# A leftover expert pair at the end of a fused attention and MoE kernel: its steps between the last units, its last rows added on chip

## The chip, the cores and the metric

One core of a Trainium2 chip. The core has TensorE (PE, with its weight loads PEld), VectorE (DVE), ScalarE (ACT), GpSimd (POOL) and SyncE (SP); DMAs are issued from queues of SP, POOL and ACT. The metric is the device time of one execution in microseconds (us).

## The reference

```python
# attention with one key/value head: q (8, 16, 384, 64), k and v (8, 1, 384, 64)
scores = (q @ k.T) / sqrt(64)
attn   = softmax(scores)                 # over the keys
x      = (attn @ v) -> (3072, 1024)      # 8 batches x 384 tokens, 16 heads x 64
# gated experts: 4 groups x 4 experts, w1 and w2 are 1024 x 1024 each
g = argmax(x @ w_group);     g_w = softmax(x @ w_group)[g]
e = argmax(x @ w_expert[g]); e_w = softmax(x @ w_expert[g])[e]
out[token] = g_w * e_w * (relu(x[token] @ w1[g, e]) @ w2[g, e])
```

Each token goes to one of 16 experts.

## The kernel before

The attention runs in 24 rounds, one for each 128 query tokens (8 batches of 384 tokens, so three rounds to a batch); the kernel's order is written out by hand and is the order of the instructions on each engine.

For every batch the kernel picks the expert that most of its first 128 tokens chose, loads that expert's w1 and w2 (POOL queue), and runs **all** 384 tokens of the batch through it, with a gate of zero for tokens that chose another. This work is cut into **units** (`moe_units`): 8 h units (w1, 8 matmuls of 384 columns, then Relu on ACT, lines L407 and L408), and 6 y units (w2, 8 matmuls of 512 columns at L415, then on ACT the eviction with the gate as scale at L416). A y unit makes 128 tokens by half of the 1024 output columns; after the second half the 128 rows are stored by SP (L436, 512 KB). `fill(n)` puts the next n units into the order; they fill PE between the attention's steps. The last batch's units come after the attention.

A pair (batch, expert) that some tokens chose, but that was not the batch's pick, is a **leftover**. `early_pair` (L508 on) finds the first such pair before the last batch is done, and its weights are loaded ahead (`leftover_w1`, `leftover_w2`, L544). Up to 32 of its tokens (`CAP`) are then done at the end:

- the batch's x is read back from DRAM (`xe`, L626), the tokens' ranks come from a prefix matmul (`pr`), and one-hot matrices `pick` (128 tokens by 32 ranks, repeated four times over 128 columns, fp32) are made (L653). `pg` (L659) gathers the gate and the token number of each rank; `gc` and `rows` (L661 to L664) are the gate and the row of the scatter, for four quarters of the output row on four groups of 32 partitions
- `pb` transposes (L681) and copies `xt` give x with tokens on the partitions; three of the last units stand between them
- `px` (L692) gathers the 32 tokens, `xc` is its copy on DVE; `ph` (L700) multiplies by w1, `hg` is its Relu on ACT (L702); `phT` (L705) transposes, `hc` is the copy on DVE (L707); `py` (L712) multiplies by w2, `yc` is the scaled copy on ACT (L714), 128 partitions (4 quarters by 32 tokens) by 256 columns
- POOL scatters `yc` to the rows of the output with an indirect DMA (L715). It waits until every earlier store to the output has landed, as it overwrites their zeros.

In before all remaining units are put ahead of `px`:

```python
    fill(len(units) - 1)
    rare = nc.values_load(rarei[0:1, 0:1], ...)
    fill(1)
    px = side([P, KO, CAP], FP32, "px")
```

`rare` (one load into a register on each engine) says whether more pairs are left or the softmax bound failed; it is zero in the profiled execution (none of the lines behind it ran), and a branch at L767 skips that part on each engine to the program's end (L858, where SP waits for all queues and the engines meet in barriers). SP waits at L767 until all its stores have landed, POOL until its DMAs have.

PSUM tiles of `side` come from a pool of three buffers in turn; `ps_m` has one, the attention's accumulator `o`.

Of the kernel before, what the change touches and what calls it, by code (L numbers as in the profile page):

```python
# [9 lines left out]
FP32 = mybir.dt.float32  # L10
# [3 lines left out]
P = 128  # L14
ACTF = mybir.ActivationFunctionType
OP = mybir.AluOpType
# [5 lines left out]
def kernel(  # L22
# [11 lines left out]
    nc = tc.nc  # L34
    B, H, S, D = q.shape
    N, Dm = out.shape
# [5 lines left out]
    ST = S // P  # L42
    KO = Dm // P
    FO = F // P
    GE = G * Eg
    scale = 1.0 / (D ** 0.5)
    NCH = 6
    CW = 512
    NFLAT = B * NCH
    NPAIR = B * GE  # L50
    CAP = 32
    QW = Dm // 4
# [4 lines left out]
    out4 = out.rearrange("n (q c) -> (n q) c", q=4)  # L57
# [18 lines left out]
    def side(shape, dtype, name):  # L76
        return ps_s.tile(shape, dtype, tag="s", name=name)
# [317 lines left out]
        nc.vector.reduce_sum(out=gs[:], in_=gm[:], axis=AX)  # L395
        gsel[b] = gs

    def moe_units(w1, w2, xb, gs_of, place, store):
        units = []
        state = {}  # L400

        def h_unit(fc):
            if fc == 0:
                state["h"] = pool.tile([P, FO, S], BF16, tag="hT", bufs=1, name="hT")
            ps = side([P, CW], FP32, "hps")
            for ko in range(KO):
                nc.tensor.matmul(out=ps[:, 0:S], lhsT=w1[:, ko, fc * P:(fc + 1) * P], rhs=xb[:, ko, :], start=(ko == 0), stop=(ko == KO - 1))  # L407
            nc.scalar.activation(out=state["h"][:, fc, :], in_=ps[:, 0:S], func=ACTF.Relu)  # L408

        def y_unit(st, nh):  # L410
            cs = slice(nh * CW, (nh + 1) * CW)
            y = place(st, cs)
            ps = side([P, CW], FP32, "yps")
            for fo in range(FO):
                nc.tensor.matmul(out=ps[:], lhsT=state["h"][:, fo, st * P:(st + 1) * P], rhs=w2[:, fo, nh * CW:(nh + 1) * CW], start=(fo == 0), stop=(fo == FO - 1))  # L415
            nc.scalar.activation(out=y, in_=ps[:], func=ACTF.Copy, scale=gs_of()[:, st:st + 1])  # L416
            store(st, cs, y)

        for fc in range(FO):
            units.append(lambda fc=fc: h_unit(fc))  # L420
        for st in range(ST):
            for nh in range(2):
                units.append(lambda st=st, nh=nh: y_unit(st, nh))
        return units

    def first_units(b):
        rows = {}

        def place(st, cs):
            if cs.start == 0:  # L430
                rows[st] = pool.tile([P, Dm], FP32, tag="y", bufs=4, name="y")
            return rows[st][:, cs]

        def store(st, cs, y):
            if cs.stop == Dm:
                nc.sync.dma_start(out=outv[b, :, st, :], in_=rows[st][:])  # L436
        return moe_units(wts[b][0], wts[b][1], xbf[b], lambda: gsel[b], place, store)

    NP = B * ST

# [10 lines left out]
    def fill(n):  # L451
        while n > 0:
            if not units:
                if begun[0] >= B or begun[0] not in wts:
                    return
                units.extend(first_units(begun[0]))
                begun[0] += 1
            units.pop(0)()
            n -= 1
            ran[0] += 1  # L460
            if ran[0] == (FO + 2 * ST) * (B - 2) + FO:
                leftover_w1()
            if ran[0] == (FO + 2 * ST) * (B - 1):
                leftover_w2()
# [43 lines left out]
    def early_pair():  # L508
        last = B - 1
        mask = pool.tile([P, GE], FP32, tag="mask", bufs=1, name="mask1")  # L510
        idf = pool.tile([P, 1], FP32, tag="idf", bufs=1, name="idf1")
        nc.vector.tensor_copy(out=idf[:], in_=choice[last][:, 0:1])
        nc.vector.tensor_scalar(out=mask[:], in0=iota16[:], scalar1=idf[:, 0:1], scalar2=None, op0=OP.is_equal)
        nc.vector.scalar_tensor_tensor(out=extra[:, last * GE:NPAIR], in0=seen[last], scalar=0.0, in1=mask[:], op0=OP.is_gt, op1=OP.subtract)
        known = pool.tile([P, 1], FP32, tag="known", bufs=1, name="known")
        nc.vector.reduce_sum(out=known[:], in_=extra[:], axis=AX)
        top = pool.tile([P, 8], FP32, tag="top", bufs=1, name="top2")
        idx = pool.tile([P, 8], U32, tag="idx2", bufs=1, name="idx2")
        nc.vector.max_with_indices(out_max=top[:], out_indices=idx[:], in_=extra[:])
        pf = pool.tile([P, 1], FP32, tag="pf", bufs=1, name="pf")  # L520
        nc.vector.tensor_copy(out=pf[:], in_=idx[:, 0:1])
        base = pool.tile([P, 1], U32, tag="base", bufs=1, name="base")
        nc.vector.tensor_scalar(out=base[:], in0=idx[:, 0:1], scalar1=NPAIR - GE, scalar2=None, op0=OP.bitwise_and)
        basef = pool.tile([P, 1], FP32, tag="basef", bufs=1, name="basef")
        nc.vector.tensor_scalar(out=basef[:], in0=base[:], scalar1=float(S // GE), scalar2=None, op0=OP.mult)
        gi = pool.tile([P, ST, 2], FP32, tag="gi", bufs=1, name="gi")
        nc.vector.tensor_scalar(out=gi[:, :, 1], in0=tokid[:], scalar1=basef[:, 0:1], scalar2=None, op0=OP.add)
        reg = nc.values_load(idx[0:1, 0:1], engines=(ET.Pool, ET.DVE, ET.SP), min_val=0, max_val=NPAIR - 1, skip_runtime_bounds_check_because="an index into 128 flags")
        leftover.update(known=known, pf=pf, gi=gi, reg=reg)

    def parts_of(pair):
        e_reg = nc.s_assert_within(pair & (GE - 1), 0, GE - 1, skip_runtime_bounds_check_because="the bits of an index below 128")
# [130 lines left out]
    rows = pool.tile([P, 1], U32, tag="rows", bufs=1, name="rows")  # L663
    nc.vector.tensor_copy(out=rows[:], in_=gc[:, 1:2])  # L664

    nc.vector.tensor_sub(out=small[:, 1:2], in0=nfl[:], in1=small[:, 0:1])
    nex = pool.tile([1, 1], I32, tag="nex", bufs=1, name="nex")
    nc.vector.tensor_copy(out=nex[:], in_=small[0:1, 1:2])
# [9 lines left out]
    for st in range(ST):  # L678
# [4 lines left out]
        nc.vector.tensor_copy(out=xt[:], in_=pb[:])  # L683
        xtok.append(xt)
        fill(1)
    fill(len(units) - 1)
    rare = nc.values_load(rarei[0:1, 0:1], min_val=0, max_val=2, skip_runtime_bounds_check_because="a sum of two comparisons")
    fill(1)
    px = side([P, KO, CAP], FP32, "px")
    for ko in range(KO):  # L690
        for st in range(ST):
# [1 line left out]
    xc = pool.tile([P, KO, CAP], BF16, tag="qT", bufs=2, name="xc")  # L693
    nc.vector.tensor_copy(out=xc[:], in_=px[:])

    w1c, w2c = leftover["w1"], leftover["w2"]
    ph = side([P, QW], FP32, "ph")
    for ko in range(KO):
# [1 line left out]
            nc.tensor.matmul(out=ph[CAP * g:CAP * g + CAP, :], lhsT=xc[:, ko, :], rhs=w1c[:, ko, g * QW:(g + 1) * QW], start=(ko == 0), stop=(ko == KO - 1), tile_position=(0, CAP * g))  # L700
    hg = pool.tile([P, QW], BF16, tag="pt", bufs=9, name="hg")
    nc.scalar.activation(out=hg[:], in_=ph[:], func=ACTF.Relu)  # L702
    phT = side([P, 2, P], BF16, "phT")
    for h in range(2):
        nc.tensor.transpose(out=phT[:, h, :], in_=hg[:, h * P:(h + 1) * P], identity=ident_bf[:])  # L705
    hc = pool.tile([P, 2, P], BF16, tag="qT", bufs=2, name="hc")
    nc.vector.tensor_copy(out=hc[:], in_=phT[:])  # L707
    py = side([P, QW], FP32, "py")
    for g in range(4):
        for h in range(2):  # L710
# [1 line left out]
                nc.tensor.matmul(out=py[CAP * c:CAP * c + CAP, :], lhsT=hc[:, h, CAP * g:CAP * g + CAP], rhs=w2c[:, 2 * g + h, c * QW:(c + 1) * QW], start=(g == 0 and h == 0), stop=(g == 3 and h == 1), tile_position=(0, CAP * c))  # L712
    yc = pool.tile([P, QW], FP32, tag="pt", bufs=9, name="yc")
    nc.scalar.activation(out=yc[:], in_=py[:], func=ACTF.Copy, scale=gc[:, 0:1])  # L714
    nc.gpsimd.indirect_dma_start(out=out4, out_offset=bass.IndirectOffsetOnAxis(ap=rows[:], axis=0), in_=yc[:], in_offset=None, bounds_check=4 * N - 1, oob_is_err=False)  # L715

    def load_pair(pair):
        e_reg, b_reg = parts_of(pair)
# [144 lines left out]
```

## Time and the profile before

| what | us |
|---|---|
| median of 3 runs | 462.71 (462.43 to 462.92) |
| the profiled execution | 463.58 |
| its span, first to last instruction | 462.0 |
| PE busy in the span | 450.8 |
| ScalarE, VectorE, GpSimd busy | 242.6, 305.7, 60.4 |
| first matmul of the last 6 y units | 439.85 |
| first matmul of px | 450.21 |
| start of the scatter on POOL | 455.58 |

The span is cut into 40 slices on the page; the clock granted to TensorE was 0.994 of full speed over the span. Durations of rows are one execution's. Ends of matmuls are modelled, so consecutive rows of PE overlap a little. A letter q behind an engine's name (SPq, POOLq) means its sequencer: branches, semaphore instructions, DMA issues.

### The profile page before, as it was taken

To read this page: it belongs to the slowest core of one execution; us is meant where nothing else is said; L and a number is where in the kernel's file an instruction comes from. 1 tells how busy PE (TensorE), PEld (TensorE's weight loads), DVE (VectorE), ACT (ScalarE), POOL (GpSimd) and SP (SyncE) were. 2 spreads that over 40 slices of the span, in tenths; PEclk is the share of its full clock that TensorE was granted. 3 is DMA by queue.
4 is the path that set the end of the run, shared out by engine and by line. 5 is a ranking of instruction groups with operands and counts; after the bars stand their busy time and mean duration, and the time that the engine had idled before them with its cause. 6 is when DMAs were issued, how large, how long until landed. Compare 5 with 4: busy or idle time off the path is not lost. (4 is left out here: it accounts for less than half of the span.)

```text
span 462.0 us, 10131 instructions
## 1 busy us (share of the span) xinstructions
PE 450.8 (98%) x4191; PEld 199.3 (43%) x4191; DVE 305.7 (66%) x483; ACT 242.6 (53%) x351; POOL 60.4 (13%) x83
## 2 busy tenths in 40 slices
PE   8999999999999999999999999999999999999992
PEld 6333444333533445343533435343443535344641
DVE  3999967964879286973779475992779564764400
ACT  2967645636366454745366364745457363623331
POOL 1004003000031002100030001300030000330000
PEclk9999999999999999999999999999999999999997
DMA  7697996998479691996759684996749712799981
GB/s 150 94 153 106 216 215 103 198 252 181 78 116 210 212 191 29 195 226 157 153 88 210 182 163 101 174 234 140 163 90 207 171 47 91 121 212 260 286 218 61
DMA packets 152165, 74.56 MB, mean 161 GB/s; under 512 B 120216, under 2 KB 138652, under 8 KB 152112
## 3 DMA queue, kind: packets, MB, share of 16 engines
q0 software_dynamic: 28416, 37.84, 47.2%
q1 hardware_dynamic: 122368, 35.68, 32.5%
q8 instruction: 35, 0.57, 0.5%
q10 hardware_dynamic: 1328, 0.33, 0.4%
q14 instruction: 18, 0.15, 0.1%
HBM read 92.62 MB, written 19.01 MB: 242 GB/s over the span
## 5 line engine op out<-in xcount | busy, mean ns | idle before, releaser
L253 ACT ACTIVATE pt<-s 128x1024 f32<-128x1024 f32 x144 | 142.1, 1026 | 67.2 <-PE s L251 66.4
L251 PE MATMUL s<-qT,kT 64*64 64x512 f32 x1152 | 142.8, 595 | 0.2 <-ACT qT L229 0.2
L290 PE MATMUL o<-pt,v 64*64 64x512 f32 x1152 | 141.0, 590 | 0.0
L261 DVE TENSOR_TENSOR presum<-presum,pt 128x1024 f32<-128x1024 f32 x96 | 116.6, 1215 | 16.3 <-ACT pt L253 10.9
L407 PE MATMUL hps<-xbf,w 128*128 128x384 bf16 x512 | 87.4, 326 | 0.0
L415 PE MATMUL yps<-w,hT 128*128 128x512 bf16 x384 | 85.4, 379 | 0.6 <-ACT y L416 0.6
L290 PEld LDWEIGHTS o<-pt,v 64*64 64x64 f32 x1152 | 43.5, 133 | 76.9 <-issue 73.2
L259 DVE TENSOR_TENSOR presum<-pt 128x1024 f32<-128x1024 f32 x24 | 29.4, 1224 | 69.3 <-ACT pt L253 68.5
L251 PEld LDWEIGHTS s<-qT,kT 64*64 64x64 f32 x1152 | 40.2, 133 | 64.3 <-issue 52.2
L416 ACT ACTIVATE y<-yps,gsel 128x512 f32<-128x512 f32 x48 | 32.6, 686 | 61.9 <-PE yps L415 49.9
L407 PEld LDWEIGHTS <-w 128*128 128x128 bf16 x512 | 48.6, 98 | 35.7 <-issue 4.1
L301 POOL CAST xbf<-xT 128x1024 bf16<-128x1024 f32 x24 | 25.0, 1041 | 280.8 <-DVE xT L300 280.8
L408 ACT ACTIVATE hT<-hps 128x384 bf16<-128x384 f32 x64 | 31.3, 488 | 51.0 <-PE hps L407 44.0
L415 PEld LDWEIGHTS <-hT 128*128 128x128 bf16 x384 | 36.8, 98 | 47.7 <-issue 4.9
L145 POOL DMA_DIRECT2D w<-in_moe_w_dram x36 | 24.8, 708 | 77.8 <-issue 58.7
L300 DVE TENSOR_TENSOR xT<-o,rinv 128x1024 f32<-128x1024 f32 x24 | 29.2, 1215 | 3.7 <-PE o L290 3.7
L280 DVE STREAM_TRANSPOSE rinv<-rc 128x1024 f32<-128x1024 f32 x24 | 29.9, 1245 | 0.8
L265 DVE TRANSPOSE_TENSOR_REDUCE fold<-presum 128x32 f32<-128x1024 f32 x24 | 29.6, 1232 | 0.0
L243 DVE STREAM_TRANSPOSE qT<-qraw 128x1024 f32<-128x1024 f32 x20 | 24.1, 1202 | 0.0
L209 ACT ACTIVATE qraw<-qraw 128x1024 f32<-128x1024 f32 x21 | 22.0, 1049 | 0.0
L318 DVE STREAM_TRANSPOSE L<-gps 128x32 f32<-128x32 f32 (+1 forms) x16 | 3.6, 227 | 17.4 <-PE gps L312 17.4
L273 PEld LDWEIGHTS sm<-fold,sel 64*64 64x64 f32 x192 | 7.2, 133 | 12.9 <-issue 12.9
(143 smaller groups left out, 158.2 us busy)
## 6 DMA issues: line engine op xcount, KB each, us to landing
w<-in_moe_w_dram POOLq DMA_DIRECT2D x36, 512.0 KB, 10.1
w<-in_moe_w_dram POOLq DMA_DIRECT2D x9, 2048.0 KB, 21.6
out_dram<-y SPq DMA_DIRECT2D x24, 512.0 KB, 2.8
qraw<-in_q_dram SPq DMA_DIRECT2D x56, 192.0 KB, 3.8
x_bf<-xbf SPq DMA_DIRECT2D x8, 768.0 KB, 4.6
v<-in_v_dram SPq DMA_DIRECT2D x16, 96.0 KB, 2.9
k<-in_k_dram SPq DMA_DIRECT2D x28, 48.0 KB, 2.6
qn<-in_q_dram SPq DMA_DIRECT2D x4, 256.0 KB, 5.0
```

Of the source, the lines that this page charges most:

```text
L251: nc.tensor.matmul(out=ps[64 * c:64 * c + 64, a, :], lhsT=kT[b][r, j * D:(j + 1) * D], rhs=qT[p][r, c * CW:(c + 1) * CW], start=True, stop ...
L253: nc.scalar.activation(out=t[:], in_=ps[:], func=ACTF.Exp, scale=scale)
L259: nc.vector.tensor_add(out=presum[p][:], in0=pt[p, 0][:], in1=pt[p, 1][:])
L261: nc.vector.tensor_add(out=presum[p][:], in0=presum[p][:], in1=pt[p, j][:])
L265: nc.vector.tensor_reduce(out=fold[p][:], in_=presum[p][:].rearrange("p a (n i) -> p (a n) i", i=32), axis=AX, op=OP.add, apply_transpose= ...
L280: nc.vector.transpose(out=t[:].rearrange("p (b i) -> p b i", i=32), in_=rc[:].rearrange("p c b -> p (c b)").unsqueeze(2).to_broadcast([P, ...
L290: nc.tensor.matmul(out=o_ps[p][64 * a:64 * a + 64, c, :], lhsT=v_sb[b][r, j, :], rhs=pt[p, j][r, a, :], start=(j == 0), stop=(j == KB - 1))
L300: nc.vector.tensor_mul(out=xT[b][:, :, ts], in0=o_ps[p][:].rearrange("p c (h n) -> p (c h) n", n=P), in1=rinv[p][:].rearrange("p (h n) -> ...
L407: nc.tensor.matmul(out=ps[:, 0:S], lhsT=w1[:, ko, fc * P:(fc + 1) * P], rhs=xb[:, ko, :], start=(ko == 0), stop=(ko == KO - 1))
L408: nc.scalar.activation(out=state["h"][:, fc, :], in_=ps[:, 0:S], func=ACTF.Relu)
L415: nc.tensor.matmul(out=ps[:], lhsT=state["h"][:, fo, st * P:(st + 1) * P], rhs=w2[:, fo, nh * CW:(nh + 1) * CW], start=(fo == 0), stop=(fo ...
L416: nc.scalar.activation(out=y, in_=ps[:], func=ACTF.Copy, scale=gs_of()[:, st:st + 1])
```

## The change

- `px` and what follows stand between the last six y units: `px`, unit 0, `ph`, unit 1, `phT`, units 2 and 3, `py`, unit 4, the rest, unit 5. The copies on DVE and ACT (`xc`, `hg`, `hc`, `yc`) are then beside a unit.
- The scatter is issued after `py`, and covers only the first 3072 - 128 tokens; so it waits for the stores up to units 2 and 3, not for the last one. The register load of `rare` comes after it on POOL.
- For the last 128 tokens (those of units 4 and 5) the leftover's rows are added on chip. `final` (in `early_pair`) is 1 where the leftover's batch is the last. `of_last` is `pick` of the batch's last 128 tokens times `final`, and is transposed on PE into the free part of `pg`'s tile and copied back by DVE, ahead of the rare flag's small steps. `spread()` stands between the matmuls of unit 4 and those of unit 5: four fp32 matmuls put the rows of `yc` back to their token (zero for other tokens), and ACT copies them to SBUF (`yl`). Units 4 and 5 are no longer evicted by ACT, but by one VectorE instruction each: PSUM times gate plus `yl`.
- Units 4 and 5 are stored in two halves of 256 KB (L437 of after).

```diff
--- before.py
+++ after.py
@@ -395,7 +395,7 @@
         nc.vector.reduce_sum(out=gs[:], in_=gm[:], axis=AX)
         gsel[b] = gs
 
-    def moe_units(w1, w2, xb, gs_of, place, store):
+    def moe_units(w1, w2, xb, gs_of, place, store, merge=None):
         units = []
         state = {}
 
@@ -413,7 +413,8 @@
             ps = side([P, CW], FP32, "yps")
             for fo in range(FO):
                 nc.tensor.matmul(out=ps[:], lhsT=state["h"][:, fo, st * P:(st + 1) * P], rhs=w2[:, fo, nh * CW:(nh + 1) * CW], start=(fo == 0), stop=(fo == FO - 1))
-            nc.scalar.activation(out=y, in_=ps[:], func=ACTF.Copy, scale=gs_of()[:, st:st + 1])
+            if merge is None or not merge(st, cs, ps, y):
+                nc.scalar.activation(out=y, in_=ps[:], func=ACTF.Copy, scale=gs_of()[:, st:st + 1])
             store(st, cs, y)
 
         for fc in range(FO):
@@ -432,9 +433,33 @@
             return rows[st][:, cs]
 
         def store(st, cs, y):
-            if cs.stop == Dm:
+            if closes(st):
+                nc.sync.dma_start(out=outv[b, :, st, cs], in_=y)
+            elif cs.stop == Dm:
                 nc.sync.dma_start(out=outv[b, :, st, :], in_=rows[st][:])
-        return moe_units(wts[b][0], wts[b][1], xbf[b], lambda: gsel[b], place, store)
+
+        def closes(st):
+            return b == B - 1 and st == ST - 1
+
+        def merge(st, cs, ps, y):
+            if not closes(st):
+                return False
+            if cs.start == 0:
+                spread()
+            nc.vector.scalar_tensor_tensor(out=y, in0=ps[:], scalar=gsel[b][:, st:st + 1], in1=leftover["y"][:, cs], op0=OP.mult, op1=OP.add)
+            return True
+        return moe_units(wts[b][0], wts[b][1], xbf[b], lambda: gsel[b], place, store, merge)
+
+    def spread():
+        lo = [ps_m.tile([P, 2, CW], FP32, tag="o", name="lo"), side([P, 2, CW], FP32, "lo2")]
+        for i in range(2):
+            for c in (i, 2 + i):
+                r = slice(CAP * c, CAP * c + CAP)
+                nc.tensor.matmul(out=lo[c // 2][:, c % 2, 0:QW], lhsT=leftover["spread"][r, :], rhs=leftover["yc"][r, :], start=True, stop=True, tile_position=(CAP * c, 0))
+        t = pool.tile([P, Dm], FP32, tag="pt", bufs=9, name="yl")
+        for i in range(2):
+            nc.scalar.copy(out=t[:, i * CW:(i + 1) * CW].rearrange("p (c n) -> p c n", c=2), in_=lo[i][:, :, 0:QW])
+        leftover["y"] = t
 
     NP = B * ST
 
@@ -525,8 +550,10 @@
         nc.vector.tensor_scalar(out=basef[:], in0=base[:], scalar1=float(S // GE), scalar2=None, op0=OP.mult)
         gi = pool.tile([P, ST, 2], FP32, tag="gi", bufs=1, name="gi")
         nc.vector.tensor_scalar(out=gi[:, :, 1], in0=tokid[:], scalar1=basef[:, 0:1], scalar2=None, op0=OP.add)
+        final = pool.tile([P, 1], FP32, tag="final", bufs=1, name="final")
+        nc.vector.tensor_scalar(out=final[:], in0=base[:], scalar1=float(NPAIR - GE), scalar2=None, op0=OP.is_equal)
         reg = nc.values_load(idx[0:1, 0:1], engines=(ET.Pool, ET.DVE, ET.SP), min_val=0, max_val=NPAIR - 1, skip_runtime_bounds_check_because="an index into 128 flags")
-        leftover.update(known=known, pf=pf, gi=gi, reg=reg)
+        leftover.update(final=final, known=known, pf=pf, gi=gi, reg=reg)
 
     def parts_of(pair):
         e_reg = nc.s_assert_within(pair & (GE - 1), 0, GE - 1, skip_runtime_bounds_check_because="the bits of an index below 128")
@@ -663,6 +690,12 @@
     rows = pool.tile([P, 1], U32, tag="rows", bufs=1, name="rows")
     nc.vector.tensor_copy(out=rows[:], in_=gc[:, 1:2])
 
+    of_last = pool.tile([P, 2, P], FP32, tag="presum", bufs=1, name="of_last")
+    nc.vector.tensor_scalar(out=of_last[:, 0, :], in0=pick[:, ST - 1, :], scalar1=leftover["final"][:, 0:1], scalar2=None, op0=OP.mult)
+    nc.tensor.transpose(out=pg[:, P:2 * P], in_=of_last[:, 0, :], identity=ident[:])
+    nc.vector.tensor_copy(out=of_last[:, 1, :], in_=pg[:, P:2 * P])
+    leftover["spread"] = of_last[:, 1, :]
+
     nc.vector.tensor_sub(out=small[:, 1:2], in0=nfl[:], in1=small[:, 0:1])
     nex = pool.tile([1, 1], I32, tag="nex", bufs=1, name="nex")
     nc.vector.tensor_copy(out=nex[:], in_=small[0:1, 1:2])
@@ -683,9 +716,7 @@
         nc.vector.tensor_copy(out=xt[:], in_=pb[:])
         xtok.append(xt)
         fill(1)
-    fill(len(units) - 1)
-    rare = nc.values_load(rarei[0:1, 0:1], min_val=0, max_val=2, skip_runtime_bounds_check_because="a sum of two comparisons")
-    fill(1)
+    fill(len(units) - 6)
     px = side([P, KO, CAP], FP32, "px")
     for ko in range(KO):
         for st in range(ST):
@@ -693,6 +724,7 @@
     xc = pool.tile([P, KO, CAP], BF16, tag="qT", bufs=2, name="xc")
     nc.vector.tensor_copy(out=xc[:], in_=px[:])
 
+    fill(1)
     w1c, w2c = leftover["w1"], leftover["w2"]
     ph = side([P, QW], FP32, "ph")
     for ko in range(KO):
@@ -700,11 +732,13 @@
             nc.tensor.matmul(out=ph[CAP * g:CAP * g + CAP, :], lhsT=xc[:, ko, :], rhs=w1c[:, ko, g * QW:(g + 1) * QW], start=(ko == 0), stop=(ko == KO - 1), tile_position=(0, CAP * g))
     hg = pool.tile([P, QW], BF16, tag="pt", bufs=9, name="hg")
     nc.scalar.activation(out=hg[:], in_=ph[:], func=ACTF.Relu)
+    fill(1)
     phT = side([P, 2, P], BF16, "phT")
     for h in range(2):
         nc.tensor.transpose(out=phT[:, h, :], in_=hg[:, h * P:(h + 1) * P], identity=ident_bf[:])
     hc = pool.tile([P, 2, P], BF16, tag="qT", bufs=2, name="hc")
     nc.vector.tensor_copy(out=hc[:], in_=phT[:])
+    fill(2)
     py = side([P, QW], FP32, "py")
     for g in range(4):
         for h in range(2):
@@ -712,7 +746,11 @@
                 nc.tensor.matmul(out=py[CAP * c:CAP * c + CAP, :], lhsT=hc[:, h, CAP * g:CAP * g + CAP], rhs=w2c[:, 2 * g + h, c * QW:(c + 1) * QW], start=(g == 0 and h == 0), stop=(g == 3 and h == 1), tile_position=(0, CAP * c))
     yc = pool.tile([P, QW], FP32, tag="pt", bufs=9, name="yc")
     nc.scalar.activation(out=yc[:], in_=py[:], func=ACTF.Copy, scale=gc[:, 0:1])
-    nc.gpsimd.indirect_dma_start(out=out4, out_offset=bass.IndirectOffsetOnAxis(ap=rows[:], axis=0), in_=yc[:], in_offset=None, bounds_check=4 * N - 1, oob_is_err=False)
+    leftover["yc"] = yc
+    nc.gpsimd.indirect_dma_start(out=out4[0:4 * (N - P)], out_offset=bass.IndirectOffsetOnAxis(ap=rows[:], axis=0), in_=yc[:], in_offset=None, bounds_check=4 * (N - P) - 1, oob_is_err=False)
+    fill(1)
+    rare = nc.values_load(rarei[0:1, 0:1], min_val=0, max_val=2, skip_runtime_bounds_check_because="a sum of two comparisons")
+    fill(1)
 
     def load_pair(pair):
         e_reg, b_reg = parts_of(pair)
```

## Prediction

> **What bounds the kernel now.** I read the page first, then the windows of the last 20 us, then the timeline from 430 us on, because every edit but one lies there; last the waits of SP and the branch line L767 and end line L858 by engine.
>
> From the page:
> ```profile
> span 462.0 us, 10131 instructions
> PE 450.8 (98%) x4191; PEld 199.3 (43%) x4191; DVE 305.7 (66%) x483; ACT 242.6 (53%) x351; POOL 60.4 (13%) x83
> ```
> TensorE (PE) has work nearly always, so a step moved to another engine early on brings nothing; only the start and the end have slack. From the windows (us, busy time of PE, PEld, DVE, ACT, POOL, clock, DMA share, GB/s):
> ```profile
> 445.00:450.00 5.00, 5.00 (x25) 2.25 (x23) 0.00 (x0) 2.06 (x3) 0.00 (x0) 1.00 0.70 243
> 450.00:455.00 5.00, 3.37 (x92) 2.39 (x90) 0.72 (x2) 1.25 (x3) 0.00 (x0) 1.00 0.28 111
> 455.00:462.00 7.00, 0.00 (x0) 0.00 (x0) 0.00 (x0) 0.29 (x1) 1.09 (x1) 0.64 0.07 22
> ```
> PE is full until 450, has holes until 455, and then there are 7 us with no compute. The timeline (start, us, engine, line) shows the holes: a chain of PE, VectorE, PE, ScalarE with nothing beside it.
> ```profile
> 450.21 0.75 PE L692 MATMUL px<-pick_bf,xt 128*128 128x32 bf16 x24
> 451.00 0.42 DVE L694 CAST xc<-px 128x256 bf16<-128x256 f32 x1 [12.86 <-PE px L692]
> 451.49 1.06 PE L700 MATMUL ph<-w,xc 128*32 128x256 bf16 x32 [0.52 <-DVE xc L694]
> 453.03 0.29 PE L705 MATMUL phT<-ident_bf,hg 128*128 128x128 bf16 x2 [0.49 <-ACT hg L702]
> 453.70 1.06 PE L712 MATMUL py<-w,hc 128*32 128x256 bf16 x32 [0.39 <-DVEq L767]
> 454.81 0.47 ACT L714 ACTIVATE yc<-py,gc 128x256 f32<-128x256 f32 x1 [1.84 <-PE py L712]
> 455.58 1.09 POOL L715 DMA_INDIRECT out_dram<-yc,rows  x1 [26.81 <-POOLq L767]
> ```
> After it comes the scatter, and then the program's end. Line L767 (the skipped branch) and L858 (the end), and SP's waits:
> ```profile
> L767 PEldq COMPARE_BRANCH  x2: 95/2007/3919, 453.8 to 455.1; - x2
> L767 SPq COMPARE_BRANCH  x2: 38/46/53, 451.5 to 454.6; - x2
> L767 POOLq COMPARE_BRANCH  x2: 38/41/44, 455.3 to 459.8; - x2
> L858 SPq EVENT_SEMAPHORE  x14: 17/28/28, 459.7 to 461.9; - x14
> L858 POOLq DRAIN  x3: 46/103/871, 460.3 to 461.7; - x3
> SPq L858 <- DMA w<-in_moe_w_dram: 5.1, 1, 5.1
> ```
> The DMA named w in SP's wait is the scatter: same software queue, issued at 455.58, landed 3.5 us later (median to landing in the issues list), so about 459.1. GpSimd (POOL) then acknowledges (INC_SWDGE_SEM at 459.4), branches at 459.8, drains 0.87 us to 461.15, and the last barrier takes 0.84 us to 461.99. The last store had landed by 454.1 (SP's branch line). So what sets the end is: chain, scatter, 2.84 us of POOL's close.
>
> **The change, part by part.** The profiled execution took 463.58 us, 1.6 around its span of 462.0; it lies 0.87 above the median of 462.71. I work out a difference on the span and apply it to the median. About 0.2% (0.9 us) is what a measurement of this kernel can tell from no change.
>
> *One more compare in early_pair* (`final`): one 128x1 DVE instruction, 0.14 us like its neighbours (L648), in the last attention round where PE has units to run. Nothing; at most 0.14 us.
>
> *The transpose of of_last behind the pg matmuls.* PE stands still here: it needs `of_last`, which DVE makes after gc, gc and rows. In the timeline these run 430.30 to 430.77; the multiply of 128x128 takes 0.345 (the first of the L653 group at 427.88) and can start at 430.69, so ends at 431.04; the transpose is a weight load of 0.14 and a matmul of 0.27 (L219). Queued behind it on PE are the h units, whose first matmul started at 430.13; it now starts at about 431.3: 1.2 us later. Part of it vanishes, since PE waited 0.42 us at 433.30 for the load of xe ("0.42 <-DMA xe" in its row), which does not depend on PE. Net **+0.8**. Below: +0.6, if the matmul ends are modelled long; above +1.2, if xe lands later too. DVE's five small steps for the rare flag slide back by a microsecond; the flag is read far later now.
>
> *The chain between the units.* px starts where y unit 0 started (439.85, now 440.65). xc (0.42) is covered by unit 0 (1.73: six units from 439.85 to 450.21), hg (0.38, behind ACT's eviction of 0.69) by unit 1, hc (0.29) by units 2 and 3. So the holes of 0.52, 0.49 and 0.39, 1.4 us, close. If the cover were gone each would return as it was. py also needs w2 of the leftover: issued 427.88, 19.6 us to landing, 447.5; py starts near 449.5, so 2 us to spare.
>
> *spread().* Four fp32 matmuls of 32 rows, 128 columns, 256 wide, in four row groups and four banks. No 32-row fp32 matmul is in the trace. Lower bound: the attention's groups of four 64x64 tiles of 512 columns (L290, 141.0 us in 144 groups) take 0.98 us, so 0.5 for 256 columns if all four run together; upper bound: four times that, 2.0, if they go one after another. I take 0.5, since four 32-wide column groups do run together in L700 (32 matmuls, 273 ns each, in 1.06 us). Its wait for yc (0.47, behind two ACT evictions) is covered by unit 4, which stands ahead of it. The two copies yl on ACT (0.69 each) are covered by unit 5.
>
> PE ends: 440.65 + 10.36 (six units) + 0.75 + 1.06 + 0.29 + 1.06 + 0.5 = 454.7; rows of different lines overlap by a tenth or two, so 454.5. Before it was 454.76: on PE nearly nothing is won, since the transpose and spread() eat the holes.
>
> *The end.* What goes is yc, POOL's scatter and its close behind PE's last matmul. What comes: the second add on VectorE. 128x1024 from PSUM takes 1.215 us (L300), so 0.61 for half, plus 0.05 to start: 455.15. SP stores 256 KB. The last store before, 512 KB, was issued at 451.1 and had landed at 454.1, 3.0 us; the shortest of the six took 2.6. I take 2.8: 458.0. SP then passes five more semaphores (0.4), branches, and reads twelve at 0.07 (459.7 to 460.5): with a jump as short as ACT's (branch 455.5, next instruction 455.9) and POOL's (459.8, 460.3) it is through at 459.7. Barrier: 0.1 and 0.84. End **460.6, a gain of 1.4**; with the overlaps and a landing of 2.6, 1.9. I forecast 1.5.
>
> *Who is next behind SP.* PE: its jump at the branch took 3.92 us from 0.36 after its last matmul; 454.5 + 4.3 = 458.8. DVE: branch 453.9, next instruction 456.8, 2.85 us: 455.2 + 3.05 = 458.2. POOL: the scatter waits until the store of units 2 and 3 has landed (they end near 449.4, eviction 0.74, store 3.0: 453.1), passes its list of waits (0.35), lands 3.57 later at 457.0; its 2.84 of close ends at 459.9. So nothing lets the gain exceed 2.2.
>
> **A rule against it.** In before, SP's jump hides in the wait of 5.1 us; now it lies on the path. DVE and PE needed 2.85 and 3.92 us for the same jump, ACT and POOL under half a microsecond. The Trainium skill (Runtime: NRT & Kernel Launch, Instruction fetch mechanics) says that a taken branch whose target is outside the two-page instruction window must first fetch it by DMA. It gives windows of 512 instructions for engines other than PE; SP's program has about 240 rows, which would put SP beside ACT and POOL and leave the sum as it is. DVE's and PE's long jumps agree with it; SP's own is shown by no row here.
>
> **The rivals.**
> - *SP's jump is a long one* (slower). If it costs DVE's 2.85 instead of 0.46, SP is through at 462.1, the end is at 463.0 and the kernel 1.0 slower; with PE's 3.92, 2.0 slower. Above a jump of about 1.9 us the change loses. For it: two of four engines pay it. Against: SP's program is the shortest, and the two that pay have the longest ones. 0.12.
> - *The PE side grows* (no change): spread() takes 2.0 instead of 0.5, or the transpose costs the whole 1.2 and the half-row store needs 3.0. Each moves the end by 0.2 to 1.5, result between 0.9 faster and 0.5 slower, most likely 0.5 faster: 462.2. 0.20.
> - *The scatter is still last* (slower). It now waits for a store issued beside other traffic; the median landing of y stores after 400 us was 5.5, not 3.0. Then it lands at 459.5, the end is at 462.4: 0.4 slower; at the longest landing, 8.2, it is 3 slower. Against: w2 has landed by 447.5, and stores issued after that needed 3.0. 0.08.
>
> **How the numbers follow.** Forecast 462.71 - 1.5 = 461.2, chance 0.60, own range 460.5 (the POOL and PE floors) to 461.8. The rivals give 462.2 (0.20), 463.7 (0.12) and 463.1 and more (0.08). The range 460.5 to 463.0 leaves out the long jump at its price and the late scatter. Faster by over 0.2% is the forecast, 0.60; within 0.2% the second rival, 0.20; slower the other two, 0.20.
>
> **What would show it.** After: PE without the three holes between px and py; a new hole of about a microsecond before the transpose at 430.3; PE's last matmul at 454 to 455; the last add ending 0.7 later; SP's last wait ended by the half-row store; the scatter landing near 457. Wrong would be: SP's first end-line semaphore over a microsecond after its branch, spread() over a microsecond, or a POOL drain that is still the last thing before the barrier.

## The result and the profile after

The changed kernel took 463.02 us (median of 6 runs, 462.64 to 463.57) beside 462.94 for the kernel before (6 runs, 462.43 to 463.28): a ratio of 1.0004, 95% interval 0.9991 to 1.0017. The forecast was 1.5 us less. The profiled execution took 463.57 us with a span of 462.1, before 463.58 with 462.0, so the two profiles can be set side by side directly.

From the page of after, its span and busy times:

```profile
span 462.1 us, 10139 instructions
PE 450.8 (98%) x4184; PEld 199.8 (43%) x4200; DVE 307.9 (67%) x488; ACT 242.3 (52%) x351; POOL 60.4 (13%) x83
```

The windows of after (us; busy time of PE, PEld, DVE, ACT, POOL; clock, DMA share, GB/s):

```profile
445.00:450.00 5.00, 4.95 (x52) 2.55 (x52) 0.29 (x1) 2.05 (x3) 0.00 (x0) 1.00 0.45 141
450.00:455.00 5.00, 4.53 (x35) 1.71 (x24) 1.05 (x2) 1.56 (x4) 1.09 (x1) 1.00 0.26 105
455.00:462.00 7.00, 0.00 (x0) 0.00 (x0) 0.45 (x1) 0.00 (x0) 0.00 (x0) 0.66 0.29 95
```

PE is full to its end now (4.53 busy from 450 to 455, and its last matmul ends at 454.58; before 3.37), the scatter has gone up beside it, and still 7 us follow with next to no compute. The DMA share of these 7 us is 0.29, before 0.07. The timeline of after (start, us, engine, line, tiles, count, idle before):

```profile
430.77 0.28 DVE L694 TENSOR_SCALAR of_last<-pick,final 128x128 f32<-128x128 f32 x1
431.10 0.33 PE L695 MATMUL pg<-ident,of_last 128*128 128x128 f32 x1 [0.76 <-DVE of_last L694]
...
442.83 1.06 PE L732 MATMUL ph<-w,xc 128*32 128x256 bf16 x32
443.82 1.90 PE L415 MATMUL yps<-w,hT 128*128 128x512 bf16 x8
...
445.56 0.28 PE L738 MATMUL phT<-ident_bf,hg 128*128 128x128 bf16 x2
...
452.04 0.71 PE L458 MATMUL lo<-yc,of_last 32*128 32x256 f32 x8
...
452.68 1.90 PE L415 MATMUL yps<-w,hT 128*128 128x512 bf16 x8
...
453.80 1.09 POOL L750 DMA_INDIRECT out_dram<-yc,rows  x1 [24.95 <-ACT yl L461]
...
454.70 0.75 DVE L449 SCALAR_TENSOR_TENSOR y<-yps,gsel,yl 128x512 f32<-128x512 f32 x1 [0.53 <-PEq L805]
```

No row between `px` and `py` waits for a copy any more. The last add ends at 455.45, and the store behind it is issued at 455.48. Then the branch line (L805 in after) with SP's waits, and the times from issue to landing of what was issued to the output from 451.5 us on (the output tile's answer; first before, where that is the scatter alone, then after):

```profile
L805 PEldq COMPARE_BRANCH  x2: 95/2294/4493, 452.1 to 454.9; - x2
L805 SPq COMPARE_BRANCH  x2: 38/46/53, 455.9 to 459.9; - x2
L805 SPq EVENT_SEMAPHORE  x9: 17/17/17, 456.0 to 459.8; - x9
L805 POOLq COMPARE_BRANCH  x2: 37/40/44, 454.0 to 459.8; - x2
SPq L805 <- SPq L805: 3.5, 3, 2.7
```
```profile
DMA to landing us min/median/max: 3.5/3.5/3.5
```
```profile
DMA to landing us min/median/max: 2.6/4.0/5.3
```

Of the three issues of after, the least (2.6) is the first half-row store, the middle one the last half-row store (4.05 us; the queue list below, which has it alone, gives it as 4.0), the most the scatter: 5.3 us, where it needed 3.5 before. So the store landed at 459.53 and the scatter at 459.07, and the program ended at 462.06.

Between them lies something that the prediction had looked at only as PE's affair. Queue q8 carries instruction pages of 16 KB. PE's jump at L805 begins at 454.92 and takes 4.49 us; its page is one packet of 1.68 us, 456.21 to 457.89 by the packet records (the second q8 packet listed begins at 460.08, behind the landings). The DMA queues and issues of after from 454.6 to 462 us, and the queues for the stretch just behind that packet (457.85 to 459.2):

```profile
q1 hardware_dynamic: 288, 0.52, 19.6%
q8 instruction: 2, 0.03, 2.5%
q14 instruction: 6, 0.05, 2.5%
q0 software_dynamic: 48, 0.06, 2.4%
out_dram<-y SPq DMA_DIRECT2D x1, 256.0 KB, 4.0
out_dram<-yc,rows POOLq DMA_INDIRECT x1, 5.3
```
```profile
DMA packets 11, 0.02 MB, mean 12 GB/s; under 512 B 3, under 2 KB 3, under 8 KB 11
q1 hardware_dynamic: 9, 0.02, 5.5%
q0 software_dynamic: 2, 0.00, 0.2%
```

All other 2 KB packets of the store had ended by 457.65. The last eight, with a completion, begin at 457.897, right behind the page, and run one after another; the scatter's last two packets stand there too (457.86 and 457.89). That they share one DMA engine with the page is inferred from this order, for the records do not name the engine. It may be a coincidence in one trace until an experiment takes the page away.

### The profile page after: what moved, and what is told of

Read it like the earlier page. It is cut to its first block, busy times and chain, and to the rows that moved or that the text cites. A ratio compares the mean times of both kernels' runs of the same rounds, so it can differ in the third digit from the quotient of the medians.

```text
span 462.1 us, 10139 instructions
## 1 busy us (share of the span) xinstructions
PE 450.8 (98%) x4184; PEld 199.8 (43%) x4200; DVE 307.9 (67%) x488; ACT 242.3 (52%) x351; POOL 60.4 (13%) x83
## 5 line engine op out<-in xcount | busy, mean ns | idle before, releaser
L417 ACT ACTIVATE y<-yps,gsel 128x512 f32<-128x512 f32 x46 | 31.3, 686 | 60.9 <-PE yps L415 49.0
```

## The experiments

Three theories stand in the expectations. **F**: the instruction page that a jump fetches near the end sits on a DMA engine in front of the last rows. **S**: the store and the scatter, now beside each other, hinder each other. **B**: the branch's own bookkeeping (compares, semaphores) costs.

All that lies ahead of the tail shifts by up to 1.1 us between the profiles (the first `pg` matmul starts at 428.79 to 429.87 us), so beside the medians I give the profile's end counted from the first `pg` matmul, and its part behind PE's last matmul:

| kernel | median us | ratio to before, 95% | end - pg | end - PE's end |
|---|---|---|---|---|
| before | 462.94 | | 32.45 | 7.23 |
| after | 463.02 | 1.0004 (0.9991 to 1.0017) | 32.44 | 7.48 |
| e1_after_norare | 460.47 | 0.9937 (0.9924 to 0.9951) | 29.11 | 4.15 |
| e2_before_norare | 460.86 | 0.9952 (0.9939 to 0.9966) | 30.20 | 5.25 |
| e14_after_small | 460.22 | 0.9938 (0.9925 to 0.9952) | 29.44 | 4.48 |
| e15_before_small | 460.79 | 0.9945 (0.9931 to 0.9958) | 29.85 | 4.85 |
| e3_noscatter | 462.24 | 0.9987 (0.9978 to 0.9997) | 31.23 | 6.27 |
| e4_onestore | 463.03 | 0.9998 (0.9990 to 1.0007) | 31.96 | 7.00 |
| e5_after_branch | 462.32 | 0.9988 (0.9979 to 0.9997) | 31.48 | 6.52 |
| e6_before_branch | 462.30 | 0.9987 (0.9978 to 0.9996) | 31.34 | 6.15 |
| e10_early_branch | 462.32 | 0.9986 (0.9977 to 0.9995) | 31.43 | 6.46 |
| e7_late | 462.02 | 0.9979 (0.9970 to 0.9987) | 31.24 | 6.81 |
| e11_early_late_branch | 461.72 | 0.9973 (0.9964 to 0.9982) | 31.09 | 6.79 |
| e13_hint_late | 461.73 | 0.9966 (0.9953 to 0.9979) | 30.70 | 6.45 |
| f1_late_hint_all | 460.91 | 0.9958 (0.9944 to 0.9971) | 29.87 | 5.59 |
| f2_before_hint_all | 462.32 | 0.9990 (0.9979 to 1.0001) | 30.83 | 5.57 |
| f3_after_hint_all | 461.51 | 0.9972 (0.9961 to 0.9984) | 30.36 | 5.39 |

(The kernel before, run again beside the experiments, took 462.85 to 463.30.)

### The skipped block taken out

```diff
-    rare_block = tc.If(rare > 0, preferred_fallthrough_block=False)
-    with rare_block:
-      ...
```

> The kernel after without the skipped part behind the branch (no branch, so no engine jumps; the output is the same as long as the flag is zero). Theory F (the fetch of PE's jump target lies on one DMA engine in front of the last rows of the store and the scatter): the last half-row store lands 2.3 to 2.9 us after its issue instead of 4.1, the scatter 3.3 to 3.8 instead of 5.3, and the span is 460.0 to 460.9, 1.2 to 2.0 below after. Theory S (store and scatter hinder each other, whatever PE does): landings of 3.8 us or more and 5 us or more stay, and the span falls by no more than 0.8, which is what the semaphore list of the branch costs SP.

> The kernel before without the skipped part. Theory F: the scatter's last rows also lay behind PE's fetch, so it lands 2.6 to 3.0 us after its issue instead of 3.6, and the span is 0.6 to 1.2 below before. Theory S: the scatter is alone here, its landing stays at 3.5, and only what the branch costs POOL goes (0.3 to 0.5).

In e1 store and scatter overlap just as in after (scatter issued 453.89, store 455.57), but nothing is fetched on q8. Landing times and queues of e1:

```profile
DMA to landing us min/median/max: 2.0/2.1/2.9
```
```profile
q1 hardware_dynamic: 288, 0.52, 19.3%
q0 software_dynamic: 48, 0.06, 2.4%
q14 instruction: 1, 0.01, 0.3%
```

The same bytes land in 2.02 us instead of 4.05, and the scatter in 2.9 instead of 5.3. S, by which the two would have stayed as slow as they were, falls as the main cause. F has the direction right, but not the size: the span fell by 3.2 us, where F gave 1.2 to 2.0. Behind PE's last matmul e1 is 3.33 us shorter, and only 2.03 of that is the store's landing. The other 1.30 lies between the landing and the program's end (2.53 us in after, 1.23 here). In after SP still has four of its nine semaphores of L805, its jump and the twelve of the end line behind the landing; in e1 the nine and the jump are gone, and six of the end line's eleven are passed before the store lands. That part fits B, not F.

e2 shows that before gains too: its scatter lands in 2.45 us instead of 3.55, and its end follows 1.98 us behind that instead of 2.87. The difference that the change makes without the skipped part is 460.47 against 460.86, not 1.5.

### The branch kept, what it skips cut to a few instructions

```diff
     with rare_block:
-      ... (the softmax repair and the loop over further pairs, with all its matmuls)
+      with tc.For_i(0, n_extra, 1) as i:   # one load, one matmul, one copy, one add to the output
+        ...
```

> The kernel after with the branch kept but little code behind it: the skipped part is cut to the list of pairs and a loop of one load, one matmul, one copy and one DMA (it does not run here, so the output is the same). Every engine still reads the flag and jumps, but over 5 to 20 instructions. Theory F (it is the fetch of the page at the jump's target that holds up the last rows): last store lands in 2.0 to 2.6 us, scatter in 2.5 to 3.2, PE's second compare takes under 0.6 us instead of 4.5, and the end is 29.0 to 30.2 us after the first pg matmul (after: 32.4; without branch: 29.1). Theory B (the branch as such costs it: flag loads, the two lists of semaphores): landings as in after, the end later than 30.8.

> The same cut of the skipped part in the kernel before. Theory F: scatter lands in 2.5 to 3.0 us, the end is 30.0 to 30.9 us after the first pg matmul (before: 32.45; without branch: 30.2), and the kernel after with the same cut is 0.3 to 1.1 us faster than this one, as without the branch. Theory B: within 0.5 of before.

The branch line of e14, and its landing times (2.4 is the last store, 3.4 the scatter):

```profile
L805 PEldq COMPARE_BRANCH  x2: 90/135/180, 451.6 to 454.5; - x2
L805 SPq COMPARE_BRANCH  x2: 38/46/53, 455.4 to 455.6; - x2
L805 SPq EVENT_SEMAPHORE  x2: 17/17/17, 455.5 to 455.6; - x2
```
```profile
DMA to landing us min/median/max: 2.4/2.9/3.4
```

All compares are there, and PE's semaphores too; PE's jump falls from 4.49 to 0.18 us, the store lands in 2.4 and the kernel is as fast as with no branch at all. So the long landing comes with the long jump, not with the branch as such. The scatter, at 3.4 us, stayed above F's 2.5 to 3.2. B is not settled by this run, since it takes bookkeeping away too: SP passes two semaphores at this line where it passed nine, and is through its jump before the store lands, so landing to end is 1.21 us, as short as in e1. The last kernel below, f3, keeps all nine. The Trainium skill (Runtime: NRT & Kernel Launch, Instruction fetch mechanics) says that a taken branch whose target is outside the two-page window first fetches the target's page; PE's 0.18 us over few instructions and 4.49 over many agree. Against before, the change is worth 0.57 us here (460.22 and 460.79).

### The scatter left out, and one store instead of two

e3 leaves the scatter out (those rows lack the leftover's part).

```diff
-    nc.gpsimd.indirect_dma_start(out=out4[0:4 * (N - P)], ...)
```

> The kernel after without the scatter (the leftover's rows outside the last 128 tokens are not written). Theory F (instruction fetches of the jumps hold a DMA engine in front of the last rows): the last half-row store still meets PE's fetch and lands 3.3 us or more after its issue; the end moves by less than 0.8 us. Theory S (scatter and store hinder each other): it lands 2.0 to 2.6 us after its issue as in the kernel without a branch, and the end comes 1.2 us or more earlier.

The store landed in 2.8 us: over the 2.0 to 2.6 of S and under the 3.3 of F, so both missed. The end came 1.2 us earlier (31.23 behind `pg`, after 32.44), which is what S had given and more than F's 0.8. PE's page took 0.98 us here instead of 1.68, and began 0.35 us after the store's issue instead of 0.73. So the page without the scatter goes with about 0.8 us over e1's 2.02; the rest of the 2 us may be the scatter's, or come of the page's length and place, which changed as well.

```diff
-            if closes(st):
-                nc.sync.dma_start(out=outv[b, :, st, cs], in_=y)
-            elif cs.stop == Dm:
+            if cs.stop == Dm:
```

> The kernel after with the last 128 rows stored once (512 KB after the second add) instead of in two halves. Theory F: with the same fetch in front and twice the bytes on the held engine, the store lands 3.5 to 5.0 us after its issue, against 4.1; end 0 to 0.8 us later than after. If the first half-row store were what holds up the second (theory S in another form), it lands in 3.0 us as the last store of before did, and the end is 0.8 us or more earlier.

No difference by the medians (0.9998), and 0.5 us earlier in the profile, between the two forecasts. The 512 KB store landed in 3.5 us. The scatter, with no half-row store issued beside it, landed in 2.6 instead of 5.3: its first packet came 1.66 us after its issue, in after 2.09, and its last ended at 455.53, early in the page's time (455.43 to 456.47). So a half-row store does delay the scatter, by some 0.4 us, but the scatter does not set the end here.

### The branch laid out the other way, and the flag loaded earlier

```diff
-    rare_block = tc.If(rare > 0, preferred_fallthrough_block=False)
+    rare_block = tc.If(rare > 0, preferred_fallthrough_block=True)
```

> The kernel after with the skipped part laid out as the next block, so that each engine jumps at the compare, which its sequencer reaches ahead of its data, and waits for its own work only behind the jump. Same work, same flags. Theory F: PE's fetch runs at 453 to 455, before the last store's rows; the store lands 2.3 to 2.9 us after its issue at about 455.5, the span is 460.2 to 461.0, 1.1 to 1.9 below after. Theory S: store and scatter land as in after (4.1, 5.3) and the span stays within 0.5 of after.

> The same edit of the branch alone in the kernel before. Theory F: PE's compare was reached at 453.85, its fetch then starts 1.2 us earlier than in before and is over before the scatter's rows come; the span falls by 0.5 to 1.0. Theory S: no change beyond 0.3.

With this layout PE has one compare instead of two, ahead of its last unit:

```profile
L805 PEldq COMPARE_BRANCH  x1: 3446/3446/3446, 451.5 to 451.5; - x1
L805 SPq COMPARE_BRANCH  x1: 50/50/50, 455.3 to 455.3; - x1
```

Its page comes at 452.44, out of the way; but the next page follows it at 455.89 (1.11 us), again ahead of the last rows: the store takes 3.64 us (F: 2.3 to 2.9), the scatter 3.9. Before and after each gain 0.6 by medians, inside F's 0.5 to 1.0 for e6 and under its 1.1 to 1.9 for e5. Moving the jump moved one fetch and left another. It also made SP's jump long, as the prediction's first rival had it: from the compare at 455.26 to the next instruction at 458.17, 2.9 us, only 0.35 ahead of the store's landing. So in e5, with SP's jump as it was, the end would hardly have come earlier without the second page.

e10 loads the flag ahead of `px` as well:

```diff
+    rare = nc.values_load(rarei[0:1, 0:1], ...)
     px = side([P, KO, CAP], FP32, "px")
     ...
-    rare = nc.values_load(rarei[0:1, 0:1], ...)
```

> The kernel after with the skipped part as the next block (as in the run of that name) and the load of the flag ahead of px, as in before. PE's sequencer then reaches the compare about a microsecond earlier than in the run with the branch edit alone (451.5), so its page and the page after it are fetched before the last store's rows at 456. Theory F: last store lands in 2.0 to 2.9 us, scatter in 2.9 to 3.6; the end is 30.0 to 31.0 us after the first pg matmul (after: 32.4, branch edit alone: 31.5); median 0.5 to 1.3 us below the branch edit alone. Theory S: no change against the branch edit alone beyond 0.3.

PE's compare stayed at 451.61: a miss. The place of the load does not set when PE's branch is taken. Store (3.02 us), scatter (3.87) and end (31.43) lie outside F's ranges too, and SP's jump ends at 458.29, behind the store's landing at 458.05: here it is SP's jump that comes last.

### The transposing behind two units

```diff
     nc.vector.tensor_scalar(out=of_last[:, 0, :], ...)
-    nc.tensor.transpose(out=pg[:, P:2 * P], in_=of_last[:, 0, :], identity=ident[:])
-    nc.vector.tensor_copy(out=of_last[:, 1, :], in_=pg[:, P:2 * P])
-    leftover["spread"] = of_last[:, 1, :]
     ...
     fill(2)
+    nc.tensor.transpose(out=pg[:, P:2 * P], in_=of_last[:, 0, :], identity=ident[:])
+    nc.vector.tensor_copy(out=of_last[:, 1, :], in_=pg[:, P:2 * P])
+    leftover["spread"] = of_last[:, 1, :]
```

> The kernel after with the transpose of of_last and its copy back moved behind the next two h units, where DVE has made of_last long before. The PE stall of 0.8 us before the transpose goes; by the trace of after against before it had moved the first pb by only 0.5 (4.25 instead of 3.76 us after the first pg matmul), the rest being the wait for xe. So PE's last matmul comes 24.5 us after the first pg matmul instead of 24.96, and the end moves by 0.3 to 0.6 us with it if the tail keeps its length of 7.5. If theory F holds, the tail's length may change by some tenths either way, since the fetch and the stores move together.

> Both edits: branch and flag load as in the run before it, and the late transpose. If they add up, the end is 0.3 to 0.6 earlier than with the branch and flag load alone, 29.5 to 30.6 us after the first pg matmul, and the median is 1.2 to 2.2 us below the kernel before.

PE's end, counted from `pg`, comes 0.53 us earlier (24.43, in after 24.96): the stall, which the prediction priced at 0.8 and which measured 0.5 in after, is recovered by order alone. The median went down by 1.0 against after, 0.5 more than PE gives; the tail behind PE was 0.67 shorter in the profile, which may be no more than where the page fell. With the layout of e5 and the early load (e11) it is 1.15 below before, just short of the 1.2 to 2.2 expected; its end, 31.09 behind `pg`, is later than the 29.5 to 30.6 expected, and its store, again beside a page (455.96 to 456.84), took 3.9 us.

### The jump announced

`mark_branch_hint_location` puts a hint of the jump at the start of the program on the engines named (in f3 the five BRANCH_PREFETCH_HINT rows stand at 0.97 to 1.10 us).

```diff
+    tc.mark_branch_hint_location("rare", hint="LikelyTaken", engines=[PE, DVE])
     ...
-    rare_block = tc.If(rare > 0, preferred_fallthrough_block=False)
+    rare_block = tc.If(rare > 0, preferred_fallthrough_block=True, label="rare")
```

> The late transpose, the skipped part as next block, and a prefetch hint for PE's and DVE's compare at the start of the kernel's main block (the flag load stays where it is in after). If the hint makes the two sequencers fetch the target page together with the page that holds the compare, PE's compare takes under 0.6 us instead of 3.4 and the end is 0.5 us or more earlier than with branch, flag load and late transpose (31.1 us after the first pg matmul). If a hint so far ahead is lost again, the compare takes 3.3 us or more as there and the end is the same within 0.4.

e13 (with the late transposing): PE's compare takes 0.48 us (e5: 3.45). Now SP's jump is last: its compare at 454.43, its next instruction at 457.30, 2.87 us later, while the store had landed at 456.7. The three kernels that follow name all five engines; f1 is e13, f2 is before and f3 is after with that hint (f2 and f3 in the layout of e6 and e5).

```diff
-    tc.mark_branch_hint_location("rare", hint="LikelyTaken", engines=[PE, DVE])
+    tc.mark_branch_hint_location("rare", hint="LikelyTaken", engines=[PE, DVE, ACT, POOL, SP])
```

> e13 with the branch hint on all five engines instead of PE and VectorE alone; whole kernel otherwise. F (a fetch near the end is what costs): SP's compare falls from 2.87 us to under 0.6, the half-row store still lands within 2.8 us of its issue, the end stands 4.2 to 5.4 us behind PE's last matmul (e13: 6.45), and the median is 1.0 to 2.0 us below e13's distance to before: 460.4 to 461.4. B (branch bookkeeping itself): no change from e13, end 6.2 to 6.7 behind PE.

> The kernel before with the branch laid out as in e6 and the hint on all five engines; nothing else changed. F: no instruction page of 8 or 16 KB is fetched behind PE's last matmul, the scatter lands within 2.7 us of its issue (before 3.5), the end is 4.9 to 5.6 us behind PE's last matmul (7.23 in before, 5.25 without the skipped part), and the median 1.5 to 2.3 us below before. B: as e6, 0.6 us below before.

> The changed kernel with the same layout and hint as f2; nothing else changed. F: the half-row store lands within 2.6 us, the scatter within 3.5, the end is 4.2 to 5.0 us behind PE's last matmul (7.48 in after), and the median lies 0.3 to 1.0 us below f2's: the change keeps its small worth in the whole program. Were the forecast's own 1.5 us to return once the fetch is gone, it would lie 1.2 to 1.8 below f2. B: 0.6 us below before, no difference from f2.

The branch line of f1, its landing times (2.6 is the first half-row store, 2.7 the last, 4.0 the scatter), and its queues from PE's end (453.64) to the program's:

```profile
L806 SPq EVENT_SEMAPHORE  x9: 17/17/17, 455.4 to 457.5; - x9
L806 PEldq COMPARE_BRANCH  x1: 482/482/482, 451.1 to 451.1; - x1
L806 SPq COMPARE_BRANCH  x1: 70/70/70, 454.9 to 454.9; - x1
```
```profile
DMA to landing us min/median/max: 2.6/2.7/4.0
```
```profile
q1 hardware_dynamic: 288, 0.52, 25.7%
q0 software_dynamic: 48, 0.06, 3.2%
q14 instruction: 4, 0.03, 2.3%
```

SP is through its jump 0.5 us after the compare (454.92 to 455.43; e13: 2.87), no 16 KB page lies behind PE's end, and the store's landing sets the end again. f1 ends 0.83 earlier than e13 in the profile; its median is 1.94 below before's, where e13 was 1.57 below. That is less than the 1.0 to 2.0 below e13 that F gave, and its end stands 5.59 us behind PE's, not 4.2 to 5.4: the store, at 2.72 us instead of e1's 2.02, is the new limit, with 1.97 us of close behind it instead of 1.23. f1 computes everything, and is faster than both kernels of the change.

f3 is the cleanest test, since it differs from e5 by the hint alone: the work, the layout and SP's nine semaphores are the same. Landing times of e5, then of f3, and SP's list in f3:

```profile
DMA to landing us min/median/max: 2.6/3.6/3.9
```
```profile
DMA to landing us min/median/max: 2.5/2.8/3.8
L806 SPq EVENT_SEMAPHORE  x9: 17/17/17, 455.8 to 457.7; - x9
```

The last half-row store is the 3.6 of e5 (3.64) and the 2.5 of f3 (2.53), and no 16 KB page lies behind PE's end in f3. The end gains from SP's jump as well, 0.5 us instead of 2.9; the landing does not depend on it. The scatter hardly moved (3.94 and 3.81, F: within 3.5). From the landing to the end f3 needs 1.97 us, where after needed 2.53 and e1 1.23: of the 1.30 that fits B, about half a microsecond was SP's jump behind the landing, and the rest stays with the lists of semaphores.

All the kernels with a last store of 256 KB agree. Six have a q8 page between the issue and the landing of that store (e3, e10, e7, e5, e11, after): it lands in 2.85 to 4.05 us, and always 1.2 to 1.7 us behind the end of the page. Five have none (e1, e14, f3, e13, f1): 2.02 to 2.72 us.

f3 lies 0.8 us below f2 by medians, and 0.47 in the profiles: inside F's 0.3 to 1.0, and well short of 1.5. The sizes by themselves missed: f3's end stands 5.39 behind PE's (expected 4.2 to 5.0), and in f2 PE's compare still took 3.19 us with the hint, and its median is only 0.53 below before's, with runs from 461.48 to 463.48 and the profile taken from a low one. In that profile PE's page came only at 457.59, behind the scatter's last packet (457.43), and the scatter landed in 2.45 us. Why the hint served PE in after and not in before stays open.

## Why the prediction was wrong

The forecast was a gain of 1.5; none was measured. The outcome is that of the second rival (no change, 0.20), but not by its mechanism: spread() took 0.64 us to the next unit, not 2.0, and the transposing 0.5, not 1.2. Its slower store points the right way, but it named 3.0 us, 0.2 over the 2.8 of the sum. By the prediction's own steps, from the profile after:

| step | predicted | measured |
|---|---|---|
| transposing, net on PE | 0.8 | 0.5 (first `pb` matmul 4.25 behind `pg`, before 3.76) |
| holes between `px` and `py` | closed | closed |
| spread(), to the next unit | 0.5 | 0.64 |
| PE's last matmul ends | 454.5 | 454.58 |
| PE's end to the add's end | 0.65 | 0.87 |
| last half-row store, issue to landing | **2.8** | **4.05** |
| scatter, issue to landing | **3.57** | **5.3** |
| SP's jump | 0.46 | 0.49 |
| landing to the program's end | 2.6 | 2.5 |
| end | 460.6 | 462.06 |

**The step that failed is the landing of the last half-row store**, taken as 2.8 from stores of twice the bytes; 1.25 of the 1.46 us by which the end was missed lie there, 0.2 in the add (0.75 us where half of 1.215 was taken). The step beside it failed too: the scatter was to land at 457.0 and let POOL be through at 459.9; it landed at 459.1, and with POOL's 2.84 of close it would have held the end at 461.9 even if the store had been in time. So two paths that I had taken as independent went late together.

What they share is PE's jump. The prediction counted it as PE's own chain (454.5 + 4.3 = 458.8, off the path), and PE itself was indeed off the path. What it left out, at a price of nothing, is that a jump of 4 us is a transfer, and that it runs among the last rows. The rows that it took for landings, 2.6 to 3.0 us, were of stores with no q8 page in flight; the one row of before that lay beside the page (456.55 to 457.52) was the scatter's 3.5, and it was taken as the scatter's price. Without the page the store took 2.0 to 2.4 us in e1 and e14 and, with the whole program, 2.53 to 2.72 in f3, e13 and f1; before's scatter took 2.45 in e2, e15 and f2.

The same runs correct the forecast's base. With the long jump out of the way the change is worth

- 0.39 us in e1 against e2 (profiles: 1.09),
- 0.57 in e14 against e15 (0.40),
- 0.81 in f3 against f2 (0.47, where f2's PE still fetched),

so 0.4 to 0.8 by medians, against 0.1 the other way, which is within the noise, with the page. The size is rough: only in the first pair do the runs of the two kernels not overlap. About 1.1 of the forecast 1.5 was the page's price in before's scatter (3.55 against 2.45 us), which the change was to escape and did not.

**What held.** SP's jump was short (0.49 us), so the first rival did not come about. e5 and e13 show that it was near: laid out the other way, SP's jump takes 2.9 us, so the prediction's argument from SP's short program does not hold in general. The third rival had the right symptom (a scatter landing at 459.1 where it asked for 459.5) with another cause: the scatter was issued at 453.80, not late, and was slow in flight. In the trace of after store and scatter landed 0.46 us apart, and both must be early for a gain.

**What is not settled.** How scatter and page share the store's delay: e3 leaves the scatter out, but there the page was also shorter and came earlier, and no run here fixes its place with all else equal. Nor why the scatter needs 3.8 to 4.0 us beside a half-row store in f3, e13 and f1, where no 16 KB page is in flight; something of S holds for it.

## What to carry to other kernels

A long jump at the end of a program is a transfer: look in the queue list for instruction pages beside the last stores, and price landings from rows that had such a page in flight. When work is moved off the last path, ask what the old path and the new one have in common; here the page held the scatter before and the scatter and the store after, and the move only changed which rows stood behind it. On PE, a rarely taken part was cheap to skip here when it was short (0.18 us) or, in three kernels of four, when the jump was announced early (0.48 us), and dear otherwise (3.3 to 5.1 us). A list of waits that stands behind the last landing costs too: 1.3 us here between after and e1.

## What the runs showed of the hardware

- A jump over a long part, not announced, cost PE 3.3 to 5.1 us, over a short one 0.18; a 16 KB page on q8 is one packet of 0.9 to 1.8 us here (one of 2.4 in e6), while the pages of the second instruction queue, q14, are packets of 8 KB (0.3 to 0.8 us).
- A 256 KB store with such a packet between issue and landing took 2.85 to 4.05 us (six kernels), without one 2.02 to 2.72 (five); in after the last eight of its 128 packets stood behind the page.
- A branch hint at the program's start cut PE's compare from 3.45 to 0.48 us and SP's jump from 2.9 to 0.5, and in one kernel did not serve PE (3.19).
- Four fp32 matmuls of 32 rows in four row groups, 256 columns wide, ran in 0.64 us together, counted to the next unit's first matmul.
